# Banks of the second chunk's transposes, an earlier first weight load, a pair of maxima and an addition moved, in a transformer block on one core

## The chip, the cores and the metric

The kernel runs on one core of one Trainium2 chip. The metric is the device time of one execution in microseconds; smaller is better. The core has five engines with a queue each: PE (matrix products; its weight loads, PEld, overlap its matmuls), DVE (vector work), ACT (activations, copies), POOL (GpSimd) and SP, which here issues nearly all DMA transfers. Each engine runs its own queue in order, and an instruction waits until the semaphores that it names are reached. Matmul results go to PSUM, eight banks of 128 partitions by 512 float32.

## What is computed

The reference, cut to the computation (S = 2048 tokens, D = 640, 32 heads of 20, a window of 256 keys, 1728 hidden units):

```python
xn = _layernorm(x, axis=-1)
return x + _A_ref(xn, A_wqkv, A_wo) + _B_ref(xn, B_w_gate, B_w_up, B_w_down)

# _A_ref: sliding-window attention
scores = jnp.einsum("bhqd,bhkd->bhqk", q, k) * (Dh ** -0.5)
mask = (idx[:, None] - idx[None, :] >= 0) & (idx[:, None] - idx[None, :] < W)
scores = jnp.where(mask[None, None], scores, -1e9)
p = _softmax(scores, axis=-1)
o = jnp.einsum("bhqk,bhkd->bhqd", p, v)
return (lambda x, *d: x.transpose(*d))(o, 0, 2, 1, 3).reshape(B, S, D) @ wo

# _B_ref: gated GELU
h = _gelu(g) * u
return jnp.einsum("bsf,fd->bsd", h, w_down)
```

All is float32. The kernel keeps that accuracy by splitting each operand of a product into a high part (rounded to the type that PE reads quickly) and a low part (the rest), and by adding three products: high by high, low by high, high by low. In names, `xh` and `xl` are the two parts of the normalised and transposed x, `wqh`/`wql` and `wvh`/`wvl` those of weights.

## The kernel before

The tokens are cut into four chunks of 512 (c = 0 to 3), each of four tiles of 128. D is cut into KT = 5 blocks of 128 (k). Four phases follow one another.

**The ramp (lines 342 to 470).** For each chunk: load four x tiles (`ln_load`), take their mean and variance on DVE (`ln_stats`, lines 141 to 143), normalise them in place (`ln_apply`, line 161), transpose them block by block on PE (`turn`, line 178), copy the result from PSUM to `xh` on ACT and form `xl` on DVE (lines 186 and 187; 349 and 346 for chunk 0). Then PE makes the first projections of q and k (`proj_qk`, matmul at line 108, into `ps_d`) and those of v (`proj_v`, into `ps_v`) for the chunk. `save_qk` splits a q or k result into three bfloat16 parts (ACT line 274, DVE line 270 into `r`, ACT line 255, POOL line 256) and stores them to DRAM; `save_v` copies v (ACT line 328).

Three PSUM pools are open in this phase: `psd` with two banks (tag "dn"), `psx` with two (tag "ex") and `psm` with four (tag "mx"). A tile takes the next bank of its pool and waits until the last reader of the tile that had it before is done. `turn` takes a letter that picks the pool: "x" for `psx`, "m" and "o" for `psm`. For chunks 1 to 3 `ln_turn` makes all five blocks; its letters alternate, x, m, x, m, x.

In chunk 0 (`first_chunk`) the order of all engines but SP is written by hand, as the code stands. It works on two halves of 256 tokens, `halves[0]` from tiles 0 and 1, `halves[1]` from tiles 2 and 3. `ta` are the transposes of the first half, `tb` those of the second. `high` makes `xh` (ACT), `low` makes `xl` (DVE), `part` issues five matmuls of one product over one half. `wr0` and `wr5` are the raw weights of q tile 0 and k tile 0; `high_qk` makes their high part (ACT, line 358), `low_qk` their low part (POOL, line 363). A copy of one element on POOL makes POOL wait until `xs[3]` is normalised. Ahead of this block PE runs 64 small matmuls on zeros (`warm`). What is not written by hand, such as POOL's memsets of the v tiles, of `ones` and of the mask, is placed by the planner: in the built order of this kernel they stand ahead of `first_chunk`'s POOL work.

For chunk 1 PE's order is written by hand too (lines 442 to 447): VLEAD = 35 matmuls of the v projections of chunk 0 (60 in all) come first, then the 20 transposes of chunk 1, then the other v matmuls.

**Attention (lines 791 to 840).** All engines but SP are in a hand-written order made by a slot loop: 32 units u (8 groups of four heads by 4 chunks), NS = 14 slots each, T counts slots. In each slot come score products and exponentials, row maxima (`max_pair`: products into two `psm` banks, line 509, read by DVE, line 513), products with v (line 595), and a measure of filler matmuls (`pull_fill`: projections for later groups and the gate and up projections). `pull_max(2, T)` takes the next two max pairs from a stream of eight per unit, that is four DVE reductions. Before slot 0 come 12 ramp slots with six such pulls, and then a stretch of filler, `pull_fill(GAP)` with GAP = 16. In the loop, pulls come at slots 0 (twice from unit 1 on), 4 and 8, and one at T = 2.

**Gate and up (lines 866 to 1380)**, and **the last phase (lines 1383 to 1453)**, which makes the output for 256 tokens at a time (p = 0 to 7) in ten steps each. A step adds into seven or so PSUM banks, named 1 to 8 by their role; from p = 1 on, a step has 21 matmuls in the bank order 1, 2, 4, 5, 6, 7, 3 (line 1208). For each step, `split_step` makes the high and low parts of the left operand two steps ahead (ACT, then DVE line 1046, ending in two low parts, "lo"). At the last step of a p (the turn), `split_step` also calls `first_copy` (bank 1 to SBUF, ACT) and `first_add` (bank 2 plus x, DVE), and `drain` adds the other banks to the x tile `xr` and stores the result; the first of its additions for p = 1 to 6 is bank 4's. The next p's matmuls on a bank wait until DVE or ACT has read it.

Of the kernel before, what the change touches and what calls it, by code (L numbers as in the profile page):

```python
# [31 lines left out]
RATE = 34.05  # L32
V1_AT = "gu", 0, 3
VEARLY = 2
VLEAD = 35
POOL_SLOTS = 13, 0, 1, 2, 3, 4, 5, 6, 7
MXD = 6
KSLOT = 9
# [30 lines left out]
def block_kernel(ctx, tc, x, wqk, wv, wgu, wdo, wdl, out):  # L69
# [64 lines left out]
    def ln_load(t, lp):  # L134
        xi = lp.tile([128, D], F32, name="xi", tag="xi", bufs=8)
        nc.sync.dma_start(xi, x[t * 128:(t + 1) * 128, :])
        return xi
# [43 lines left out]
    def ln_turn(t0, xs):  # L181
        n = len(xs)
        cs = slice(t0 * 128, (t0 + n) * 128)
        for k in range(KT):
            ps = turn(k, xs, "xm"[k % 2])
            nc.scalar.activation(xh[:, k, cs], ps, AF.Copy)
            nc.vector.tensor_tensor(out=xl[:, k, cs], in0=ps, in1=xh[:, k, cs].bitcast(F32), op=OP.subtract)

# [153 lines left out]
    def first_chunk(xs, wr0, wr5, lp):  # L342
        halves = slice(0, 256), slice(256, 512)

        def low(k, ps, cs):
            nc.vector.tensor_tensor(out=xl[:, k, cs], in0=ps, in1=xh[:, k, cs].bitcast(F32), op=OP.subtract)

        def high(k, ps, cs):
            nc.scalar.activation(xh[:, k, cs], ps, AF.Copy)

        def part(ps, w, r, cs, first=False, last=False):
            for k in range(KT):
                nc.tensor.matmul(ps[:, cs], w[:, k, :], r[:, k, cs], start=first and k == 0,
                                 stop=last and k == KT - 1, skip_group_check=True)

        def high_qk(raw):
            wh = wp.tile([128, KT, 128], F32R, name="wqh", tag="wqh")
            nc.scalar.activation(wh, raw, AF.Copy)
            return wh

        def low_qk(raw, wh):
            wl = wp.tile([128, KT, 128], F32R, name="wql", tag="wql")
            nc.gpsimd.tensor_tensor(out=wl, in0=raw, in1=wh.bitcast(F32), op=OP.subtract)
            return wh, wl

        with tc.manual_schedule(engines=MANUAL | {mybir.EngineType.Pool}):
            mv = [lp.tile([128, 2, 2], F32, name="mv", tag="mv", bufs=2) for _ in range(2)]
            ln_stats(xs[0], mv[0][:, 0, :], lp)
            ln_stats(xs[1], mv[0][:, 1, :], lp)
            rs = ln_rstd(*ln_sqrt(mv[0], 2, lp), 2, lp)  # L370
            ln_apply(xs[0], mv[0][:, 0, :], rs[:, 0:1])
            ln_apply(xs[1], mv[0][:, 1, :], rs[:, 1:2])
            ln_stats(xs[2], mv[1][:, 0, :], lp)
            ln_stats(xs[3], mv[1][:, 1, :], lp)
            ta = [turn(k, xs[0:2], "xmxmm"[k]) for k in range(KT)]
            dn = [psd.tile([128, C], F32, name="ps_d", tag="dn") for _ in range(2)]
            high(0, ta[0], halves[0])
            wh0 = high_qk(wr0)
            high(1, ta[1], halves[0])
            wh5 = high_qk(wr5)  # L380
            high(2, ta[2], halves[0])
            vb = ln_sqrt(mv[1], 2, lp)
            for k in (3, 4):
                high(k, ta[k], halves[0])
            for k in range(2):
                low(k, ta[k], halves[0])
            rs = ln_rstd(*vb, 2, lp)
            ln_apply(xs[2], mv[1][:, 0, :], rs[:, 0:1])
            ln_apply(xs[3], mv[1][:, 1, :], rs[:, 1:2])
            part(dn[0], wh0, xh, halves[0], True)  # L390
            part(dn[1], wh5, xh, halves[0], True)
            nc.gpsimd.tensor_copy(one[:, 0:1], xs[3][:, 0:1])
            w0, w5 = low_qk(wr0, wh0), low_qk(wr5, wh5)
            tb = [turn(0, xs[2:4], "o")]
            for k in range(2, KT):
                low(k, ta[k], halves[0])
            for k in range(1, KT):
                tb.append(turn(k, xs[2:4], "oxmxm"[k]))
            for k in range(KT):
                high(k, tb[k], halves[1])  # L400
            for k in range(KT):
                low(k, tb[k], halves[1])
            mv = lp.tile([128, 4, 2], F32, name="mv4", tag="mv4", bufs=2)
            part(dn[0], wh0, xl, halves[0])
            part(dn[1], wh5, xl, halves[0])
            part(dn[0], wh0, xh, halves[1])
            part(dn[1], wh5, xh, halves[1])
            for i, w in enumerate((w0, w5)):
                part(dn[i], w[1], xh, halves[0])
                part(dn[i], w[1], xh, halves[1])  # L410
                part(dn[i], w[0], xl, halves[1], last=True)
                for j in range(4 if i == 0 else 0):
                    ln_stats(xs[4 + j], mv[:, j, :], lp)
                save_qk(5 * i, 0, dn[i])
        return w0, w5, mv

    v0 = []
    with tc.tile_pool(name="lp", bufs=1, side="right") as lp:
        xs = [ln_load(t, lp) for t in range(4)]
        warm = lp.tile([128, 256], BF, name="warm")[:, 0:128]  # L420
        nc.vector.memset(warm, 0.0)
        ps = psd.tile([128, C], F32, name="ps_u", tag="dn")
        for i in range(WARM):
            nc.tensor.matmul(ps[:, 0:128], warm, warm, start=True, stop=True)
        wr0, wr5 = load_qk(0), load_qk(5)
        prep = load_v(0, v0, lp)
        next(prep)
        xs += [ln_load(t, lp) for t in range(4, 8)]
        w0, w5, mv1 = first_chunk(xs, wr0, wr5, lp)
        run(prep)  # L430
        v0 = v0[0]
        ones = lp.tile([4, 2 * C], BF, name="ones")
        nc.gpsimd.memset(ones, 0.0)
        nc.gpsimd.memset(ones[0:2], 1.0)
        for i in range(NK):
            for j in (0, 2):
                nc.sync.dma_start(ks[i][SR:64, j:j + 2].rearrange("p j t -> p (j t)"), ones)
        for c in range(1, NC):
            ln_scale(xs[4 * c:4 * c + 4], lp, mv1 if c == 1 else None)
            vs = [proj_v(v0, 4 * c - 4 + i, None if i % 2 else (psm, "mx")) for i in range(4)]  # L440
            if c == 1:
                with tc.manual_schedule(engines={mybir.EngineType.PE}):
                    lead = (cost for gen in vs for cost in gen)
                    for _ in range(VLEAD):
                        next(lead)
                    ln_turn(4 * c, xs[4 * c:4 * c + 4])
                    run(lead)
            else:
                ln_turn(4 * c, xs[4 * c:4 * c + 4])
            if c + 1 < NC:  # L450
                xs += [ln_load(t, lp) for t in range(4 * c + 4, 4 * c + 8)]
            if c == 1:
                for i in range(NQ):
                    for j in (0, 2):
                        nc.sync.dma_start(qs[i][SR + 2:64, j:j + 2].rearrange("p j t -> p (j t)"), ones[2:4])
            if c == 2:
                band = lp.tile([128, D], F32, name="xi", tag="xi", bufs=8)[:, 0:320]
                for t, shift in ((mask, 0), (band, 64)):
                    nc.gpsimd.memset(t, 0.0)
                    nc.gpsimd.affine_select(out=t, in_=t, pattern=[[1, 320]], compare_op=OP.is_ge,  # L460
                                            fill=NEG, base=shift - 1, channel_multiplier=-1)
                    nc.gpsimd.affine_select(out=t, in_=t, pattern=[[-1, 320]], compare_op=OP.is_ge,
                                            fill=NEG, base=256 - shift, channel_multiplier=1)
                nc.gpsimd.tensor_copy(mask[64:128], band[64:128])
                raws1 = [load_qk(1), load_qk(6)]
            if c < NC - 1:
                run(*vs)
                run(proj_qk(0, w0, c), proj_qk(5, w5, c))
            else:
                run(*[proj_v(v0, 4 * c - 4 + i) for i in range(VEARLY)])  # L470
# [320 lines left out]
    def attention():  # L791
# [7 lines left out]
        for i in range(12):  # L799
# [4 lines left out]
                pull_max(2, now[0])  # L804
            flush()
            pull_fill(2 * RAMP)
        pull_fill(GAP)
        for u in range(NU + 1):
            for i in range(NS):
                T = now[0] = NS * u + i  # L810
                for fn, a in tick():
                    fn(*a)
                if i in (0, 4, 8) or T == 2:
                    pull_max(2, T)
                if i == 0 and u:
                    av_unit(u - 1)
# [405 lines left out]

    def first_add(ps, xt):
        sub(xt[:, 1, 0:HD], ps[2][:, 0:HD], xt[:, 1, 0:HD], OP.add)

    puts = []

    def drain(p, ps, xt):
# [21 lines left out]
        if p == NP - 1:  # L1250
# [13 lines left out]
            add(1, 2, b[3])  # L1264
            store(1, 2)
            return
        add(2, 1, b[4])
        sub(q, b[6], a, OP.add)
        add(1, 2, q)
        sub(q, b[7], q, OP.add)  # L1270
# [226 lines left out]
```

## Time and profile before

| | |
|---|---|
| time, median of 3 runs | 1053.38 us (1052.72 to 1054.26) |
| the profiled execution | 1051.12 us |
| its span in the trace | 1049.4 us |
| DVE, ACT, POOL busy | 730.4, 515.1, 333.4 us |
| maxima on DVE (line 513) | 512, 474 ns each |
| DMA, read and written | 101.78 MB, 54.92 MB |

The profile is of one execution. Each row of its timeline has a start, a duration (of all instructions of the row together), the engine, the source line, the operation, output and inputs by the program's names, the shape and the count; in square brackets stands how long the engine was idle before it and what ended the idle time. Rows merge instructions of one line, so a row of 16 transposes is 16 instructions. A matmul's end is modelled and includes its latency, so consecutive rows of PE overlap a little; for the pace of PE one takes the distance between starts. A wait for several semaphores is put down to the one that came last by the trace.

### The profile page before, as it was taken

How to read it: one execution, taken by the hardware profiler on the slowest of the kernel's cores; microseconds unless marked ns; L12 is line 12 of the kernel's file. 1: busy time of each engine (PE TensorE's matmuls, PEld its weight loads, DVE VectorE, ACT ScalarE, POOL GpSimd, SP SyncE). 2: the span in 40 equal slices, each digit the busy share in tenths (PEclk: the TensorE clock that was granted, in tenths of full speed). 3: DMA queues.
4: the chain of work that ended last, by engine and by line, in shares of the span. 5: the costliest groups of instructions: out<-in, count | busy, mean ns of one | idle time of the engine just before them, and what ended most of it. 6: DMA issues, size and time to landing. Idle time of an engine off the chain costs nothing.

```text
span 1049.4 us, 22713 instructions
## 1 busy us (share of the span) xinstructions
PE 1037.5 (99%) x7997; PEld 826.7 (79%) x7997; DVE 730.4 (70%) x2007; ACT 515.1 (49%) x1088; POOL 333.4 (32%) x502
## 2 busy tenths in 40 slices
PE   8999999999999999999999999999999999999998
PEld 7887666666677766666666888888888999999998
DVE  8745656666665556677672677877656889888887
ACT  4434667666665566656555622222334554333332
POOL 5121676867373548373735011110110000000000
PEclk9999999999999999999999999999999999999999
DMA  6543455655443244444322656676317874443442
GB/s 212 181 118 97 122 154 157 180 170 168 119 127 98 85 116 142 152 124 136 107 84 67 196 186 243 211 251 239 119 51 256 267 247 136 132 130 112 126 136 92
DMA packets 105179, 158.56 MB, mean 151 GB/s; under 512 B 15420, under 2 KB 60092, under 8 KB 105064
## 3 DMA queue, kind: packets, MB, share of 16 engines
q1 hardware_dynamic: 102680, 150.95, 45.5%
q10 hardware_dynamic: 2384, 6.16, 1.9%
q8 instruction: 63, 1.03, 0.4%
q14 instruction: 52, 0.43, 0.1%
HBM read 101.78 MB, written 54.92 MB: 149 GB/s over the span
## 4 chain that ended last, share of the span: by engine, by line
PE 93%; DVE 4%; issue 1%; DMA 1%; ACT 1%; POOL 0%; SPq 0%; DVEq 0%; POOLq 0%
PE ps_d L108 21%; PE ps L1208 21%; PE ps_g L941 21%; PE ps_e L568 8%; PE ps_o L595 8%; PE ps_v L108 6%; PE ps_m L509 5%; PE ps_g L108 1%; DVE xi L161 1%; DVE st L142 1%; DVE st L141 1%; DVE ss L1046 0%; DVE junk L513 0%; DVE r L270 0%; DMA qs<-qd 0%
## 5 line engine op out<-in xcount | busy, mean ns | idle before, releaser
L513 DVE CUSTOM_DVE_ANT_0 junk<-ps_m,mask 128x320 bf16<-128x320 f32 (+2 forms) x512 | 242.9, 474 | 146.5 <-PE ps_m L509 88.2
L570 ACT ACTIVATE P<-ps_e 128x512 f32<-128x512 f32 (+2 forms) x384 | 198.2, 569 | 66.4 <-PE ps_e L568 62.0
L1208 PE MATMUL ps<-wb,at 128*128 128x320 f32 x999 | 155.9, 309 | 0.0
L1208 PEld LDWEIGHTS ps<-wb,at 128*128 128x128 f32 x999 | 148.9, 188 | 0.2
L581 POOL TENSOR_SCALAR_AFFINE_SELECT P<-P 128x512 f32<-128x512 f32 x128 | 83.5, 652 | 153.3 <-ACT P L570 153.3
L568 PE MATMUL ps_e<-qs,ks 124*128 124x128 bf16 (+2 forms) x704 | 117.3, 278 | 0.3 <-ACT ob L599 0.2
L108 PE MATMUL ps_d<-xh,wqh 128*128 128x512 f32 x350 | 107.8, 416 | 0.0
L108 PE MATMUL ps_d<-xl,wqh 128*128 128x512 f32 x350 | 107.5, 415 | 0.0
L108 PE MATMUL ps_d<-xh,wql 128*128 128x512 f32 x350 | 107.2, 414 | 0.0
L1208 PE MATMUL ps<-wt,at 128*128 128x320 f32 x552 | 89.1, 309 | 0.5 <-DVE xr L1233 0.5
L568 PEld LDWEIGHTS <-ks 124*128 124x128 bf16 x704 | 49.4, 98 | 48.0 <-issue 33.6
L595 PE MATMUL ps_o<-P,v 128*32 128x384 f32 (+2 forms) x1408 | 84.3, 386 | 0.0
L1208 PEld LDWEIGHTS ps<-wt,at 128*128 128x128 f32 x552 | 82.9, 188 | 0.9 <-DVE xr L1233 0.7
L1162 ACT ACTIVATE at<-ss 128x512 fp32r<-128x512 f32 x59 | 37.3, 632 | 89.3 <-DVE ss L1046 89.3
L584 POOL TENSOR_SCALAR_AFFINE_SELECT P<-P 128x512 f32<-128x512 f32 x112 | 72.7, 659 | 25.1 <-ACT P L570 25.1
L101 POOL TENSOR_TENSOR wql<-wr,wqh 128x640 fp32r<-128x640 f32 x11 | 17.6, 1607 | 174.8 <-PE ps_g L941 129.4
L108 PEld LDWEIGHTS ps_d<-xh,wql 128*128 128x128 f32 x350 | 64.2, 189 | 10.5
L108 PEld LDWEIGHTS ps_d<-xl,wqh 128*128 128x128 f32 x350 | 64.1, 189 | 10.4 <-issue 0.2
L108 PEld LDWEIGHTS ps_d<-xh,wqh 128*128 128x128 f32 x350 | 63.7, 189 | 10.4 <-issue 0.3
L595 PEld LDWEIGHTS ps_o<-P,v 128*32 128x32 f32 x1408 | 41.3, 110 | 38.6 <-issue 21.9
L256 POOL TENSOR_TENSOR pt<-r,pt 128x512 bf16<-128x512 f32 x40 | 46.8, 1170 | 66.7 <-ACT pt L255 52.6
L509 PE MATMUL ps_m<-ks,qs 60*64 60x320 bf16 (+2 forms) x1472 | 62.2, 260 | 2.1 <-DVE mx L513 1.0
(193 smaller groups left out, 1808.0 us busy)
## 6 DMA issues: line engine op xcount, KB each, us to landing
hr<-hd SPq DMA_DIRECT2D x104, 128.0 KB
hd<-he SPq DMA_DIRECT2D x50, 256.0 KB
wr<-wgu SPq DMA_DIRECT2D x27, 320.0 KB
qs<-qd SPq DMA_DIRECT2D x64, 120.0 KB
ks<-kd SPq DMA_DIRECT2D x64, 120.0 KB
xi<-x SPq DMA_DIRECT2D x16, 320.0 KB
qs<-qd SPq DMA_DIRECT2D x64, 80.0 KB
ks<-kd SPq DMA_DIRECT2D x64, 80.0 KB
```

What stands on the lines that cost most here:

```text
L108: nc.tensor.matmul(ps, a(k), b(k), start=n == 0, stop=n == 3 * nk - 1)
L256: nc.gpsimd.tensor_tensor(out=pt[:, l, :], in0=r, in1=pt[:, 1, :], op=OP.subtract)
L509: nc.tensor.matmul(ps[64 * h:64 * h + 64, lo:hi], q[rows, j, q0:q0 + 64], keys, start=True, stop=True, tile_position=(64 * r, 64 * h))
L513: nc.vector.tensor_tensor_reduce(out=junk[:, 0:n], in0=ps[:, 0:n], in1=mask[:, 320 - n:320], scale=1.0, scalar=NEG, op0=OP.add, op1=OP.max ...
L568: nc.tensor.matmul(ps[:, col:col + n], k[0:QROWS, j, kc:kc + 128], q[0:QROWS, j, q0:q0 + n], start=True, stop=True)
L570: nc.scalar.activation(pt[:, j, lo:hi], ps[:, lo:hi], AF.Exp, scale=SCALE)
L581: nc.gpsimd.affine_select(out=a, in_=a, pattern=[[0, 4], [1, 128]], compare_op=OP.is_ge, fill=0.0, base=0, channel_multiplier=-1)
L584: nc.gpsimd.affine_select(out=a, in_=a, pattern=[[0, 4], [-1, 128]], compare_op=OP.is_ge, fill=0.0, base=-1, channel_multiplier=1)
L595: nc.tensor.matmul(o[32 * j:32 * j + 32, q0:q0 + n], v[:, w0_:w0_ + 32], pt[:, j, col:col + n], start=i == 0, stop=i == len(todo) - 1, ski ...
L941: nc.tensor.matmul(ps, i, j, start=first and n == 0, stop=n == len(work) - 1, skip_group_check=True)
L1162: nc.scalar.activation(hi[:, 3:7], s, AF.Copy)
L1208: nc.tensor.matmul(ps[bank][:, 0:HD], *work[bank][j], start=bank not in begun, stop=final[p, bank] == n and j == len(work[bank]) - 1, skip ...
```

## The change

Four edits, in one diff:

1. `ln_turn` picks the pools by "xmmxm" instead of x, m, x, m, x, and VLEAD goes from 35 to 40.
2. The load of `wr0` is issued after the first two x tiles instead of after four. In `first_chunk`, `wh0` is made (ACT) ahead of the `xh` copies and `w0`'s low part (POOL) right behind it, after a one-element copy that makes POOL wait for `xs[1]`; `wh5` comes after the fourth `xh` copy. The product of `w0`'s low part with the first half is issued second instead of late.
3. One `pull_max(2)` moves from T = 2 to the middle of the gap ahead of slot 0.
4. In the last phase the addition of bank 4 moves from the start of `drain` to `first_add`, that is ahead of the two low parts of `split_step`.

```diff
-VLEAD = 35
+VLEAD = 40
...
-            ps = turn(k, xs, "xm"[k % 2])
+            ps = turn(k, xs, "xmmxm"[k])
...
             ln_stats(xs[3], mv[1][:, 1, :], lp)
+            nc.gpsimd.tensor_copy(one[:, 0:1], xs[1][:, 0:1])
+            wh0 = high_qk(wr0)
+            w0 = low_qk(wr0, wh0)
             ta = [turn(k, xs[0:2], "xmxmm"[k]) for k in range(KT)]
             dn = [psd.tile([128, C], F32, name="ps_d", tag="dn") for _ in range(2)]
             high(0, ta[0], halves[0])
-            wh0 = high_qk(wr0)
-            high(1, ta[1], halves[0])
+            for k in range(1, 4):
+                high(k, ta[k], halves[0])
             wh5 = high_qk(wr5)
-            high(2, ta[2], halves[0])
             vb = ln_sqrt(mv[1], 2, lp)
-            for k in (3, 4):
-                high(k, ta[k], halves[0])
+            high(4, ta[4], halves[0])
...
             part(dn[0], wh0, xh, halves[0], True)
+            part(dn[0], w0[1], xh, halves[0])
             part(dn[1], wh5, xh, halves[0], True)
             nc.gpsimd.tensor_copy(one[:, 0:1], xs[3][:, 0:1])
-            w0, w5 = low_qk(wr0, wh0), low_qk(wr5, wh5)
+            w5 = low_qk(wr5, wh5)
...
             for i, w in enumerate((w0, w5)):
-                part(dn[i], w[1], xh, halves[0])
+                if i:
+                    part(dn[i], w[1], xh, halves[0])
                 part(dn[i], w[1], xh, halves[1])
...
-        xs = [ln_load(t, lp) for t in range(4)]
+        xs = [ln_load(t, lp) for t in range(2)]
+        wr0 = load_qk(0)
+        xs += [ln_load(t, lp) for t in range(2, 4)]
...
-        wr0, wr5 = load_qk(0), load_qk(5)
+        wr5 = load_qk(5)
...
-        pull_fill(GAP)
+        pull_fill(GAP / 2)
+        pull_max(2, now[0])
+        pull_fill(GAP / 2)
...
-                if i in (0, 4, 8) or T == 2:
+                if i in (0, 4, 8):
                     pull_max(2, T)
...
     def first_add(ps, xt):
         sub(xt[:, 1, 0:HD], ps[2][:, 0:HD], xt[:, 1, 0:HD], OP.add)
+        sub(xt[:, 0, 0:HD], ps[4][:, 0:HD], xt[:, 0, 0:HD], OP.add)
...
-        add(2, 1, b[4])
         sub(q, b[6], a, OP.add)
```

In the built order of the changed kernel, the one-element copy and `w0`'s low part stand on POOL ahead of the memsets of the v tiles, `ones` and the mask. On SP, the x tiles 10 and 11 are loaded behind the stores of the first q and k results (before, tile 11 alone), and each of the second weight loads comes behind a pair of stores. On DVE, two of chunk 2's tiles have their statistics ahead of chunk 1's `xl`, and two behind them.

## The prediction, made before the changed kernel was run

> **What bounds the kernel now.** I read the page first, then busy time by stage, then the waits of PE, then the timeline at each place that an edit touches.
>
> ```profile
> span 1049.4 us, 22713 instructions
> ...
> PE 1037.5 (99%) x7997; PEld 826.7 (79%) x7997; DVE 730.4 (70%) x2007; ACT 515.1 (49%) x1088; POOL 333.4 (32%) x502
> ...
> PE 93%; DVE 4%; issue 1%; DMA 1%; ACT 1%; POOL 0%; SPq 0%; DVEq 0%; POOLq 0%
> ```
>
> ```profile
> 0.00:13.50 13.50, 9.51 (x85) 8.05 (x85) 9.29 (x32) 6.62 (x16) 6.27 (x24) 1.00 0.83 303
> ...
> 25.70:33.30 7.60, 6.14 (x48) 5.81 (x46) 7.27 (x21) 3.68 (x11) 0.00 (x0) 1.00 0.53 144
> ...
> 65.00:110.00 45.00, 44.09 (x347) 33.76 (x349) 23.80 (x94) 18.37 (x55) 12.24 (x13) 1.00 0.39 117
> 110.00:820.00 710.00, 708.52 (x5711) 513.71 (x5704) 464.85 (x1363) 377.25 (x780) 299.68 (x450) 1.00 0.48 152
> ```
>
> The first fence has the span, the engines and the chain's shares of the page; the second has stages (start:end, length, then busy us of PE, PEld, DVE, ACT, POOL, granted clock, DMA share, GB/s). PE is 99% busy and 93% of the chain that ended last, at full clock. Both kernels have the same number of matmuls, so only idle PE time can be won: span less PE's busy time is 11.9 us. Four of them lie ahead of 13.5 us, 1.5 in 25.7 to 33.3 (which ends where the first ps_d of chunk 1 starts), 0.9 in 65 to 110, 1.5 in the next 710. What ended that idle time:
>
> ```profile
> PE ps_t L178 <- DVE xi L161: 1.9, 2, 1.2
> PE ps_t L178 <- DVE xl L187: 1.5, 1, 1.5
> ...
> PE ps_m L509 <- DVE mx L513: 1.0, 3, 0.4
> PE ps_m L509 <- DMA qs<-qd: 0.9, 1, 0.9
> ...
> PE ps L1208 <- DVE xr L1233: 0.5, 1, 0.5
> ...
> PEld ps_t L178 <- DVE xl L187: 2.4, 3, 1.7
> ```
>
> Columns: us in total, times, longest. The four edits touch the waits on xl, xi, mx and xr.
>
> **Edit 1, the banks (ln_turn, VLEAD).** Before, the five transposes of a chunk alternate between pool x (two banks) and pool m, so k=4 needs k=0's bank and waits for DVE's xl of k=0. With "xmmxm" x serves k=0 and 3, m serves k=1, 2 and 4. These three and the two v projections in m are five uses of four banks; the one used twice in chunk 1 is that of the first v tile, which ACT has saved long before. So the wait goes in chunks 1, 2 and 3:
>
> ```profile
> 25.70 1.97 PE L178 MATMUL ps_t<-ident,xi 128*128 128x128 f32 x16
> ...
> 29.14 0.42 PEld L178 LDWEIGHTS ps_t<-ident,xi 128*128 128x128 f32 x4 [1.70 <-DVE xl L187]
> ...
> 42.41 0.42 PEld L178 LDWEIGHTS ps_t<-ident,xi 128*128 128x128 f32 x4 [0.35 <-DVE xl L187]
> ```
>
> The weight-load side gives the fuller stall, since a matmul's modelled end includes its latency: 1.70 + 0.35, and by the total of 2.4 for three another 0.35 in chunk 3. Bounds: 1.5 (PE's own row) to 2.4 gained; I take **-2.4**, because PE's next instruction starts when its weights are in. VLEAD 40 puts five more v matmuls ahead of chunk 1's transposes, 0.147 us each (35 of them from 20.57, a row below, to 25.70): 0.73 moved, not added. What is late next is DVE's normalising of chunk 1, done at 25.98 (23.48 + 2.50 below), and the five matmuls cover it. In chunks 2 and 3 the second v projection now asks for a bank that DVE frees with r; in DVE's order that r comes ahead of xl of k=0, the very wait removed, and PE has the rest of the transposes and 15 matmuls (2.2 us) ahead of it: nothing added.
>
> **Edit 2, the first weights.** On SP the load of wr0 goes ahead of x tiles 2 and 3; ACT makes wqh0 before the xh copies; POOL waits for xs[1] (the one-element copy), makes wql0, and only then runs the memsets and masks it used to run at the start; five wql0 matmuls (first half) move ahead of xs[3].
>
> ```profile
> 13.53 1.20 PE L178 MATMUL ps_t<-ident,xi 128*128 128x128 f32 x9 [0.74 <-DVE xi L161]
> 16.97 1.36 PE L353 MATMUL ps_d<-xh,wql 128*128 128x256 f32 x10
> 18.17 0.76 PE L353 MATMUL ps_d<-xl,wqh 128*128 128x256 f32 x5
> 20.57 0.90 PE L108 MATMUL ps_v<-wvh,xh 128*128 128x320 f32 x5
> ```
>
> ```profile
> 1.79 0.11 POOL L309 MEMSET v<- 128x12 f32 x1
> ...
> 3.61 0.94 POOL L434 MEMSET ones<- 2x1024 bf16 x1
> ...
> 5.02 0.45 POOL L462 TENSOR_SCALAR_AFFINE_SELECT mask<-mask 128x320 f32<-128x320 f32 x1
> ...
> 15.12 3.10 POOL L363 TENSOR_TENSOR wql<-wr,wqh 128x640 fp32r<-128x640 f32 x2
> ```
>
> Ten wql matmuls take 18.17 - 16.97 = 1.20, so five are worth 0.60, and PE sits idle for 0.74 just ahead of xs[3]: they fit. POOL pays for it. xs[1] is ready at 8.18 (7.05 + 1.13 below) and wql0 lasts 1.55 (half of 3.10), so it is done at 9.9; the memsets and the first mask step take 5.02 - 1.79 = 3.2, to 13.1; three wvl, the second mask step and the gate follow, and wql5 is done at about 18.3. PE asks for it at 18.17 (five wql0 fewer, the five xl now ahead of it): a wait of 0.1. That leaves -0.5.
>
> Against it, the moved POOL work now lies under DVE's two normalising steps of tiles 2 and 3:
>
> ```profile
> 7.05 1.13 DVE L161 TENSOR_SCALAR xi<-xi,mv,rs 128x640 f32<-128x640 f32 x2
> ...
> 11.79 1.68 DVE L161 TENSOR_SCALAR xi<-xi,mv,rs 128x640 f32<-128x640 f32 x2
> ...
> 21.44 1.17 POOL L256 TENSOR_TENSOR pt<-r,pt 128x512 bf16<-128x512 f32 x1 [1.54 <-ACT pt L255]
> 21.48 1.48 DVE L161 TENSOR_SCALAR xi<-xi,mv,rs 128x640 f32<-128x640 f32 x1
> ...
> 23.48 2.50 DVE L161 TENSOR_SCALAR xi<-xi,mv,rs 128x640 f32<-128x640 f32 x3
> ```
>
> ```profile
> 99.72 0.64 POOL L584 TENSOR_SCALAR_AFFINE_SELECT P<-P 128x512 f32<-128x512 f32 x1
> ...
> 100.11 0.27 DVE L522 TENSOR_SCALAR nm<-mx 128x16 bf16<-128x16 f32 x1
> ```
>
> Alone, two steps take 1.13. Behind POOL's 1.17 one step takes 1.48 and ends 0.35 after POOL's op; the small tensor_scalar at 100.11 ends at 100.38, with POOL's select (100.36). No row shows a POOL memset under such a step. If it blocks nothing, the two steps take 1.13 instead of 1.68 and -0.5 stands. If it blocks as the select does, the first step waits for the 0.90 of ones (11.74 to 12.64), the second for a select, and they end at about 14.2 instead of 13.47; POOL slips too, wql5 is done at about 18.95, and PE reaches the v projections at 18.95 + 0.05 + 15 x 0.12 = 20.8 against 20.57: +0.25. DVE's chunk 1 is then ready at 26.7, and PE starts its transposes at 25.70 + 0.25 + 0.73 = 26.7. A memset is nearest to the select's row: I take **+0.1**, toward that end; bounds -0.6 and +1.0 (each step behind a 0.9 us op, and wql5 late by as much).
>
> [...]
>
> Late elsewhere, at no cost: x tiles 2 and 3 come behind 320 KB more, but DVE asks for tile 2 only after 8.18. The eight ks<-ones transfers stand on SP until the later memset of ones (12.6 instead of 4.55), and x loads of chunk 2 queue behind them and behind the q and k stores; DVE asks for two of those tiles at 25.98, for the other two only after the xl of chunk 1. If that cover failed, chunk 2's normalising would be late by what the tiles miss.
>
> **Edit 3, the pair of maxima.** One pull (two pairs) moves from slot T=2 to the middle of the gap, where DVE is idle.
>
> ```profile
> 94.69 0.47 PE L509 MATMUL ps_m<-ks,qs 60*64 60x64 bf16 x16
> 95.07 0.49 DVE L513 CUSTOM_DVE_ANT_0 junk<-ps_m,mask 128x320 bf16<-128x320 f32 x1 [4.63 <-PE ps_m L509]
> ...
> 96.70 0.51 PE L509 MATMUL ps_m<-ks,qs 60*64 60x320 bf16 x5
> ...
> 97.56 0.33 PE L509 MATMUL ps_m<-ks,qs 60*64 60x320 bf16 x3 [0.35 <-DVE mx L513]
> ...
> 100.13 0.33 PE L509 MATMUL ps_m<-ks,qs 60*64 60x128 bf16 x7 [0.28 <-DVE mx L513]
> ```
>
> Three pulls fall within 5 us, DVE lags, and PE waits 0.35 + 0.28. After, the third comes 5 us after the second, so 0.28 goes. The first two are then 12 v matmuls and the pull's own 0.47 apart, 2.2 us against 2.0 now, so about 0.15 of the 0.35 stays. **-0.45**; bounds -0.63 and +0.3 (the wait stays, with one more like it).
>
> **Edit 4, the addition.** add(2,1,b4) goes ahead of DVE's two lo splits at six turns; at one of them PE waits now:
>
> ```profile
> 901.90 2.22 PE L1208 MATMUL ps<-wt,at 128*128 128x320 f32 x12 [0.46 <-DVE xr L1233]
> ...
> 902.87 0.49 DVE L1046 TENSOR_TENSOR u<-ps,u 128x320 f32<-128x320 f32 x1
> ...
> 903.42 0.45 PEld L1208 LDWEIGHTS ps<-wt,at 128*128 128x128 f32 x3 [0.20 <-DVE u L1046]
> ```
>
> Bank 4 comes free about 1 us earlier, so the 0.46 goes. But DVE has the same work ahead of its read of bank 7 (902.87), which ends at 903.36 as now, and PE, at bank 7 earlier, waits there until 903.42: the stall moves by nine matmuls, its end stands. **0**; bounds -0.46 and +0.1. The lo splits come one addition later; the 21 matmuls of a whole step (3.1 us) stand ahead of their use.
>
> **Sum**: -2.4 + 0.1 - 0.45 + 0 = -2.75 us. The profiled execution took 1051.12 (span 1049.4, 1.7 around it), 2.26 under the median 1053.38; the three timed runs spread over 1.5 us. Span 1046.65, that execution 1048.4, median **1050.6 us** (-0.26%). After 110 us PE's progress releases nearly everything else, so I expect it to keep its lead.
>
> **Rivals.** (a) POOL takes the gain of the ramp: its ops block both normalising steps and wql5 is late, +1.0 instead of +0.1, and chunk 1's transposes wait 0.4 more for DVE. Gain 1.45: 1051.9. For: 1.48 behind 1.17. Against: at 11.79, with POOL's wvl beneath, DVE lost only 0.55 over its two steps (1.68 against 1.13).
> (b) The bank stall is hidden anyway: PE gains 1.7 in chunk 1 and loses it again behind DVE's r and xl, which the first maxima need. Gain 1.05: 1052.3. For: DVE is busy 7.27 of 7.60 there. Against: in 65 to 110 DVE is busy only half the time.
> (c) Slower: the stack loads (qs<-qd) keep their time while PE is 2.75 ahead, so that maxima find their data late. It decides from the fourth further wait of 0.9 on; six make +5.4, net +2.65: 1056.0. For: one such wait exists. Against: it is alone among 32 units, and the loads are released by PE's own progress.
>
> Chances: forecast 0.62, (a) 0.2, (b) 0.11, (c) 0.07. The measurement tells 0.2% (2.1 us) from no change: the forecast counts as faster, (a) and (b) as within it. Range: the low ends together, -0.6 - 2.4 - 0.63 - 0.46 = -4.1, give 1049.3; (b) with 0.4 of spread gives 1052.7.
>
> **What would show it.** Right: no wait of ps_t on xl; five wql matmuls ahead of xs[3]; the first ps_d of chunk 1 at about 31.6 instead of 33.3; no wait at T=4; at the turn near 899 one wait of about 0.7 on bank 7 in place of two. L161 near 12 us decides on the memsets: 1.1 for the pair without a lock, over 2 with it, and then the second wql group waits for POOL. Wrong: PE's idle time after 110 us grows by over 1 us, or that ps_d starts after 32.5.

## The result, and the profile after

The changed kernel took **1047.88 us** (median of 6 runs, 1047.34 to 1048.98), before in the same comparison 1053.79 (6 runs, 1052.72 to 1054.88): ratio 0.9945, 95% interval 0.9932 to 0.9958. The forecast was 1050.6, its range 1049.3 to 1052.7: right in sign, but the measured time lies 1.4 us below the range. The profiled executions stand closer together, 1051.12 before and 1047.46 after. So there are two questions: why the trace shows 3.7 us instead of the 2.75 of the sum, and where the other 2.2 us between 3.7 and 5.9 are.

The page of the changed kernel, its span, busy times and the chain's shares:

```profile
span 1045.7 us, 22718 instructions
...
PE 1035.9 (99%) x7997; PEld 826.6 (79%) x7997; DVE 730.8 (70%) x2007; ACT 514.7 (49%) x1088; POOL 333.6 (32%) x503
...
PE 96%; DVE 2%; DMA 1%; ACT 0%; issue 0%; SPq 0%; DVEq 0%
```

Its stages, columns as before:

```profile
0.00:13.50 13.50, 9.41 (x90) 8.31 (x90) 9.26 (x31) 6.79 (x16) 6.35 (x24) 1.00 0.83 302
...
25.70:31.23 5.53, 5.53 (x45) 5.52 (x44) 5.50 (x13) 3.10 (x9) 0.22 (x1) 1.00 0.65 194
65.00:110.00 45.00, 44.64 (x359) 33.68 (x358) 25.15 (x97) 20.28 (x56) 12.50 (x13) 1.00 0.39 119
110.00:820.00 710.00, 708.82 (x5701) 515.87 (x5700) 465.38 (x1356) 375.22 (x777) 299.52 (x449) 1.00 0.48 152
```

What PE waited for (total, times, longest):

```profile
PE ps_t L178 <- DVE xi L161: 2.4, 3, 1.5
...
PE ps_m L514 <- DMA qs<-qd: 0.6, 1, 0.6
PE ps L1215 <- DVE u L1053: 0.4, 1, 0.4
PE ps_m L514 <- DVE mx L518: 0.4, 1, 0.4
```

No wait on xl is left, the waits on mx fell from 1.0 to 0.4, and that on xr became one on u. The waits on xi rose from 1.9 to 2.4, of which 0.3 is only that the warm-up row ended earlier (1.48 idle behind it instead of 1.17) while the first transposes start where they did (7.84 and 7.81). PE has no idle time from 25.7 to 31.23; the stretch from 110 to 820 is as full as before. Its timeline in the ramp (start, duration, instruction):

```profile
11.21 0.75 PE L353 MATMUL ps_d<-xh,wql 128*128 128x256 f32 x5
...
13.17 0.33 PE L178 MATMUL ps_t<-ident,xi 128*128 128x128 f32 x1 [0.62 <-DVE xi L161]
...
20.26 0.90 PE L108 MATMUL ps_v<-wvh,xh 128*128 128x320 f32 x5
...
26.13 2.34 PE L178 MATMUL ps_t<-ident,xi 128*128 128x128 f32 x20
...
31.23 1.32 PE L108 MATMUL ps_d<-xh,wqh 128*128 128x512 f32 x5
```

The five wql matmuls stand at 11.21, ahead of the transposes of xs[2] and xs[3]; the 20 transposes of chunk 1 run in one piece; the first ps_d of chunk 1 starts at 31.23. Landmarks along PE, from the two timelines, us:

| where | before | after | lead |
|---|---|---|---|
| v projections start | 20.57 | 20.26 | 0.31 |
| first ps_d of chunk 1 | 33.30 | 31.23 | 2.07 |
| first ps_m | 65.23 | 62.56 | 2.67 |
| first ps_n | 86.16 | 83.46 | 2.70 |
| pull at T=14 (slot 0 of unit 1) | 108.23 | 104.46 | 3.77 |
| end of the span | 1049.4 | 1045.7 | 3.7 |

Edits 1 and 2 give 2.7 by 63 us, edit 3 gives 1.07 between 86 and 108, and from there on the lead stays.

### The profile page after: what moved, and what is told of

Read it like the earlier page. It is cut to its first block, busy times and chain, and to the rows that moved or that the text cites. A ratio compares the mean times of both kernels' runs of the same rounds, so it can differ in the third digit from the quotient of the medians.

```text
span 1045.7 us, 22718 instructions
## 1 busy us (share of the span) xinstructions
PE 1035.9 (99%) x7997; PEld 826.6 (79%) x7997; DVE 730.8 (70%) x2007; ACT 514.7 (49%) x1088; POOL 333.6 (32%) x503
## 4 chain that ended last, share of the span: by engine, by line
PE 96%; DVE 2%; DMA 1%; ACT 0%; issue 0%; SPq 0%; DVEq 0%
PE ps_d L108 23%; PE ps_g L948 21%; PE ps L1215 21%; PE ps_e L573 9%; PE ps_o L600 8%; PE ps_v L108 7%; PE ps_m L514 5%; PE ps_g L108 1%; PE ps_t L178 1%; PE ps_d L353 1%; DVE ss L1053 0%; DMA qs<-qd 0%; DVE at L1053 0%; DVE xi L161 0%; DMA xi<-x 0%
## 5 line engine op out<-in xcount | busy, mean ns | idle before, releaser
L604 ACT ACTIVATE ob<-ps_o 128x512 f32<-128x512 f32 x32 | 19.1, 597 | 88.9 <-PE ps_o L600 77.6
```

## The experiments

Each kernel was timed beside before on one chip, in four comparisons: base_again, e1_banks, e2_weights and e3_pull in the first; after_again, without_e2, before_filled and e4_add in the second; after_third and ones_first in the third; load_order and filled_again in the fourth. "Clock" is the mean granted clock of TensorE that each run lists; the last two columns are the share of runs at 0.999 or more and the median of these. The ratio is the record's estimate with its interval, not the quotient of the two medians. Before's share differs much from one comparison to the next, so shares are best compared within one.

| kernel | median us (runs) | ratio to before, 95% | at 0.999 or more | their median |
|---|---|---|---|---|
| before, four comparisons | 1053.53, 1052.58, 1053.26, 1052.07 (35, 29, 12, 23) | | 51 of 99 (14 of 35, 21 of 29, 3 of 12, 13 of 23) | 1051.88 |
| base_again | 1052.38 (12) | 0.9988, 0.9977 to 0.9999 | 8 of 12 | 1051.66 |
| e1_banks | 1050.53 (12) | 0.9972, 0.9959 to 0.9985 | 5 of 12 | 1049.59 |
| e2_weights | 1051.74 (12) | 0.9981, 0.9969 to 0.9993 | 11 of 12 | 1051.69 |
| e3_pull | 1051.74 (12) | 0.9981, 0.9968 to 0.9994 | 5 of 12 | 1050.55 |
| e4_add | 1053.32 (12) | 1.0004, 0.9992 to 1.0016 | 8 of 12 | 1051.98 |
| without_e2 | 1050.48 (11) | 0.9975, 0.9963 to 0.9986 | 4 of 11 | 1047.78 |
| after_again | 1048.62 (5) | 0.9956, 0.9942 to 0.9970 | 5 of 5 | 1048.62 |
| after_third | 1048.91 (7) | 0.9960, 0.9945 to 0.9974 | 6 of 7 | 1048.61 |
| ones_first | 1049.50 (5) | 0.9959, 0.9947 to 0.9972 | 4 of 5 | 1049.16 |
| before_filled | 1052.49 (11) | 0.9999, 0.9988 to 1.0010 | 10 of 11 | 1052.41 |
| filled_again | 1052.94 (12) | 0.9996, 0.9983 to 1.0010 | 9 of 12 | 1052.10 |
| load_order | 1052.92 (12) | 1.0005, 0.9993 to 1.0017 | 6 of 12 | 1052.26 |

**base_again: before, unchanged.**

> The kernel before, unchanged, to see what a further execution of it looks like. The profiled execution of before took 1051.12 us, under all six of its timed runs (1052.72 to 1054.88), so the two profiles differ by 3.7 us where the medians differ by 5.9. Theory 1 (the profiled execution of before lacked a stall that a typical one has): a second profile is 1052.5 to 1054.5 and shows 2 us more of idle PE at one place or a few. Theory 2 (a profile of this kernel is always about 2 us under its timed runs): a second profile is again near 1051 with the same waits of PE. Ratio to before: 1.000.

The unchanged copy came out at 0.9988. A ratio nearer to 1 than about 0.0012 is therefore scatter here. Its profiled execution took 1051.37 with the same waits, as in Theory 2; but a profiled execution is not always the shorter one (that of e4_add took 1055.55, its median is 1053.32). The longer runs mostly go with a lower clock, which is taken up below.

**e1_banks: edit 1 alone.**

```diff
-VLEAD = 35
+VLEAD = 40
-            ps = turn(k, xs, "xm"[k % 2])
+            ps = turn(k, xs, "xmmxm"[k])
```

> Edit 1 alone: the letters xmmxm and VLEAD 40. By the terms of the trace it gains 2.1 to 2.4 us (the three waits on xl): 1051.4 to 1051.7 against 1053.8. If what the typical run of before has over its profile lies in these waits, 4 to 4.6 us: 1049.3.

Timelines of PE, first base_again, then e1_banks: the first ps_d of chunk 1 and the first ps_m.

```profile
33.39 1.32 PE L108 MATMUL ps_d<-xh,wqh 128*128 128x512 f32 x5
...
65.33 0.36 PE L509 MATMUL ps_m<-ks,qs 60*64 60x64 bf16 x12
```

```profile
26.53 2.35 PE L178 MATMUL ps_t<-ident,xi 128*128 128x128 f32 x20
...
31.64 1.32 PE L108 MATMUL ps_d<-xh,wqh 128*128 128x512 f32 x5
...
62.96 0.36 PE L509 MATMUL ps_m<-ks,qs 60*64 60x64 bf16 x12
```

1.75 in chunk 1 and 2.37 by the first ps_m, against 2.4 forecast. At 0.999 or more its runs are 2.07 under the copy's.

**banks_only and vlead_only: its two halves** (one of the diff's two lines each). Each ran once, under the profiler: 1051.27 and 1051.36 us, both at a clock of 0.998.

> Edit 1 without its VLEAD part (35 as before). Theory (the bank is the whole stall, VLEAD only covers DVE's normalising): no wait of ps_t on xl; PE asks for chunk 1's transposes at 25.8, DVE is done at 26.0, so at most 0.3 us of wait on xi comes in; the first ps_d of chunk 1 starts at 31.6 to 31.9, against 33.4 in before's copy and 31.64 with both parts. Rival (VLEAD carries part of the gain): 32.2 or later.

> The other part of edit 1 alone (VLEAD 40, banks as before). DVE's xl of k=0 stands behind statistics of later tiles until 28.5, whenever PE's transposes come, so the stall on it ends at 29.2 as in before; but five v matmuls (0.73 us) are then ahead of it instead of behind. Theory: the wait of ps_t on xl shrinks from 1.5 to about 0.8, the first ps_d of chunk 1 starts at 32.6 to 32.9 instead of 33.4. Rival (the stall only moves, as the transposes come later): 33.3 or later.

In both executions the clock dropped ahead of this place (below), so distances from the start of the v projections are compared. PE of banks_only, then of vlead_only:

```profile
21.92 0.90 PE L108 MATMUL ps_v<-wvh,xh 128*128 128x320 f32 x5
...
27.05 2.34 PE L178 MATMUL ps_t<-ident,xi 128*128 128x128 f32 x20
...
32.90 1.32 PE L108 MATMUL ps_d<-xh,wqh 128*128 128x512 f32 x5
```

```profile
22.20 0.90 PE L108 MATMUL ps_v<-wvh,xh 128*128 128x320 f32 x5
...
30.57 0.66 PE L178 MATMUL ps_t<-ident,xi 128*128 128x128 f32 x4 [0.59 <-DVE xl L187]
...
33.99 1.32 PE L108 MATMUL ps_d<-xh,wqh 128*128 128x512 f32 x5
```

banks_only needs 10.98 from the v projections to ps_d, as e1_banks does (31.64 - 20.66), with no wait on xl: in these executions the banks are the whole gain. The times in its expectation were those of full clock and did not come. But PE came 1.3 us late to the transposes, so whether VLEAD is needed to cover DVE's normalising at full clock was not seen. vlead_only needs 11.79, base_again 12.73. e3_pull, which has the old banks, VLEAD 35 and the same lateness, needs 12.33 (34.61 - 22.28): VLEAD alone is worth some 0.5, the low end of the 0.5 to 0.8 expected, though DVE's xl moved with the lateness (29.88 instead of 28.51), which the expectation had excluded.

**e2_weights: edit 2 alone** (its lines of the diff).

> Edit 2 alone: wr0 loaded third, wql0 ahead of the memsets, its first-half product moved up. By the trace of after PE reaches the v projections 0.31 us earlier: 0.3 us of gain, not to be told from none (1053.5); the wait of 1.5 us on xl stays. If the missing 2 us are this edit's, 1051.3.

At full clock 1051.69, level with the copy, so a gain of 0.3 can't be told from none; by its trace the v projections start at 20.29 instead of 20.66. Its clock share, 11 of 12, stands out.

**e3_pull: edit 3 alone.**

```diff
-        pull_fill(GAP)
+        pull_fill(GAP / 2)
+        pull_max(2, now[0])
+        pull_fill(GAP / 2)
...
-                if i in (0, 4, 8) or T == 2:
+                if i in (0, 4, 8):
```

> Edit 3 alone: the pull of two pairs from T=2 to the middle of the gap. The trace of after against before gains 0.9 us between the last ramp pull and the first ob copy, against 0.45 forecast: 1052.9. If DVE's backlog of maxima is worse in a typical run of before than in its profile, up to 3 us: 1050.8.

From the first ps_n to the pull at T=14 it takes 21.00 (87.47 to 108.47), the copy 22.08 (86.26 to 108.34): 1.08 gained, as in the changed kernel.

**e4_add: edit 4 alone.**

```diff
         sub(xt[:, 1, 0:HD], ps[2][:, 0:HD], xt[:, 1, 0:HD], OP.add)
+        sub(xt[:, 0, 0:HD], ps[4][:, 0:HD], xt[:, 0, 0:HD], OP.add)
...
-        add(2, 1, b[4])
```

> Edit 4 alone: the addition from bank 4 moved ahead of the first writes. Theory: the wait of 0.4 us on bank 4's reader is gone and the next one, on bank 7's reader, takes its place with 0.4 us, so the time at 1.000 is before's (1051.4 to 1052.0) and about half of the runs are at 1.000. Rival: the wait vanishes and the kernel is 0.4 us shorter at 1.000 (1051.3 or less).

PE at the turn near 900 waits on bank 7's reader and on nothing else, and the time at full clock is that of before:

```profile
905.69 1.73 PE L1208 MATMUL ps<-wt,at 128*128 128x320 f32 x9
907.84 0.71 PE L1208 MATMUL ps<-wt,at 128*128 128x320 f32 x3 [0.42 <-DVE u L1046]
```

**ones_first: the changed kernel with the two memsets of ones ahead of POOL's wait.**

```diff
+            nc.gpsimd.memset(ones, 0.0)
+            nc.gpsimd.memset(ones[0:2], 1.0)
             nc.gpsimd.tensor_copy(one[:, 0:1], xs[1][:, 0:1])
...
-        nc.gpsimd.memset(ones, 0.0)
-        nc.gpsimd.memset(ones[0:2], 1.0)
```

> The changed kernel with the two memsets of ones ahead of POOL's wait for xs[1]. In the changed kernel's profile DVE's two normalising steps for tiles 2 and 3 (L161 near 11.8) take 1.96 us; the first lies beside the memset of ones (11.82 to 12.76), the second beside the select of mask (12.74 to 13.43). Theory (a POOL memset holds back such a step): with ones out of the way the pair takes at most 1.7 (as in before, with wvl beneath it), the transposes of xs[2] start at 12.5 to 12.7 instead of 13.17, the v projections 0.2 to 0.4 earlier (19.9 to 20.1 instead of 20.26), and the profiled execution, if its clock is 1.000, is 0.2 to 0.4 shorter than the changed kernel's, too little for the medians to tell. Rival (memsets block nothing, the pair is slow for another reason): 1.9 to 2.0 again, transposes at 13.1 to 13.2.

DVE's and POOL's timelines in the changed kernel, then in ones_first:

```profile
11.81 1.96 DVE L161 TENSOR_SCALAR xi<-xi,mv,rs 128x640 f32<-128x640 f32 x2
...
11.82 0.94 POOL L439 MEMSET ones<- 2x1024 bf16 x1
12.74 0.69 POOL L465 TENSOR_SCALAR_AFFINE_SELECT mask<-mask 128x320 f32<-128x320 f32 x1
```

```profile
11.87 2.28 DVE L161 TENSOR_SCALAR xi<-xi,mv,rs 128x640 f32<-128x640 f32 x2
...
11.86 1.94 POOL L299 TENSOR_TENSOR wvl<-wvall,wvh 128x320 fp32r<-128x320 f32 x2 [0.58 <-ACT wvh L298]
```

A miss: the pair took 2.28, not 1.7, and the v projections start at 20.64, not at 19.9 to 20.1. With the memsets gone, wvl moved up into their place, 0.01 us ahead of DVE. Memset, select or wvl, the outcome is the same: of the changed kernel's pair, the first step ends at 13.12 (1.31 long), 0.36 after the memset, and the second at 13.77, 0.34 after the select; the pair in ones_first ends 0.35 after the second wvl (14.15 against 13.80). So the memset held back such a step here, and so did the select and wvl: the pairs took 1.96 and 2.28, against 1.13 with no POOL work beside them (7.05 in before). In before the pair took 1.68: its first step began 0.2 ahead of wvl and took 0.61, and only the second, 1.16 long, was held.

**The clock.** The next three kernels ask where the 2.2 us between trace and medians are.

> All four edits, timed beside before on one chip. Each run lists the mean clock granted to TensorE. At 1.000, before took 1051.9 (median of 13 runs) and its unchanged copy 1051.7 (8 runs); a run at 0.998 or below was some 2 us longer. Theory (clock): the edits save 3.7 us of work, which is what the two profiled executions differ by (both at 1.000), and the rest of the 5.9 us between the medians is runs of before whose clock fell in the ramp. So at 1.000 this kernel takes 1047.8 to 1048.4, 3.5 to 3.9 less than before at 1.000, and at least 8 of 12 runs are at 1.000, against 13 of 35 of before: the three kernels without edit 2 had 18 of 36 at 1.000, edit 2 alone 10 of 12. Rival A (the gain is larger than the profile shows): also at 1.000 the two are 5.5 to 6 us apart. Rival B (the clock is chance of the day, no edit touches it): 4 to 6 of 12 at 1.000, and the medians of all runs 3.7 apart.

> Edits 1, 3 and 4 without edit 2 (first weights loaded and split as before). Theory (clock by edit 2): about half of the runs at 1.000, as before; at 1.000 the kernel takes 1048.2 to 1048.7, that is the 0.3 us by which edit 2 brings the v projections forward more than all four edits; median over all runs 1049.3 to 1050.5. Rival (edit 2 has nothing to do with the clock): share at 1.000 and median as of the kernel with all four, within 0.4 us.

> Before, with 24 matmuls of the zero warm-up tile put into the three idle stretches of TensorE between 9.5 and 13.6 us (4 of them in the 0.23 us, 8 in the 0.51 us, 12 in the 0.74 us; 0.056 us each by the warm-up row), nothing else changed. One profile with a clock of 0.998 shows where it fell: 0.50 from 14 to 17 us, one stretch of about 3.4 us, right behind these idle stretches. Theory (the clock falls because TensorE idles there): at 1.000 in at least 9 of 12 runs, time at 1.000 unchanged (1051.4 to 1052.0), median of all runs there too, 0.5 to 1.5 us below before's. Rival (the fall has another cause, or these gaps are too small a share): 4 to 6 of 12 at 1.000, median as before's, 1052.4 to 1053.5.

Where the clock fell, in e3_pull (mean 0.998), by stages; the clock is the third number from the end:

```profile
12.00:14.00 2.00, 1.25 (x10) 0.94 (x9) 2.00 (x4) 1.44 (x5) 1.91 (x2) 0.99 0.47 177
14.00:15.00 1.00, 1.00 (x7) 1.00 (x6) 1.00 (x4) 0.92 (x3) 1.00 (x2) 0.50 0.11 27
...
16.00:17.00 1.00, 1.00 (x7) 1.00 (x6) 1.00 (x4) 0.02 (x1) 1.00 (x2) 0.50 0.79 202
17.00:18.00 1.00, 1.00 (x9) 1.00 (x9) 0.96 (x4) 0.00 (x0) 1.00 (x1) 0.81 0.77 200
```

By these means, with the clock taken as either 1.00 or 0.50 (0.99 is 0.04 us at half clock, 0.81 is 0.38), PE runs at half clock from 13.96 to 17.38; the v projections start at 22.28 instead of 20.66. e4_add (13.04 to 19.86, worked out in the same way), banks_only and vlead_only show the drop at the same place, and these four are all the profiled executions below 0.999 of kernels without fillers. Over all runs, 87 of 172 without edit 2 and without fillers were at 0.999 or more, with edit 2 32 of 35. Before's runs below it take 1054.03 (48 runs), those above 1051.88 (51): **2.15 us**. after_again missed its expected 1047.8 to 1048.4 by 0.2; without_e2 reached 1047.78 at full clock, below its expected 1048.2 to 1048.7, so the 0.3 of edit 2 does not show in the times there; over all runs it took 1050.48, because 7 of its 11 fell below.

before_filled put 24 zero matmuls into PE's idle stretches (4 after the first transposes, 8 after the second wqh matmul, 12 between the transposes of xs[2] and xs[3]). The clock held in 10 of 11 (before beside it: 21 of 29), but no time was won. So the gain, the clock and edit 2's halves were asked once more.

> The changed kernel once more, beside before on the same chip, for the two open numbers. The gain: 4 us between the medians (3.2 to 4.8), as in the second comparison (1052.58 and 1048.62), not 5.9. The clock: with edit 2 in the kernel 22 of 23 runs so far were granted 0.999 or more, without it 65 of 123 (before and its variants); so at least 10 of 12 here, and 15 to 22 of some 30 of before. Rival: shares alike.

> Before with the load of wr0 moved ahead of x tiles 2 and 3 and nothing else of edit 2: ACT, POOL and TensorE in the old order. So far 32 of 35 runs with the whole of edit 2 were granted 0.999 or more, and 68 of 137 without it. Theory (what keeps the clock is TensorE's new order around 9.5 to 13.6 us: four matmuls without a gap, five wql matmuls ahead of xs[3]): about half at 0.999 or more, as without edit 2, and the v projections start where they did in the copy of before (20.6 to 20.9 at full clock). Rival (the load order alone does it, through what the DMAs or ACT do there): at least 9 of 12.

> Before with the 24 zero matmuls in TensorE's three idle stretches, once more: 10 of 11 runs were at 0.999 or more, but their median was 0.5 us above that of before's runs at such a clock, and the overall median no lower than before's. Theory (the idle stretches cause the drop, and the 0.5 us was scatter): at least 9 of 12 again, median 0.5 to 1.3 us below before's of the same chip. Rival 1 (10 of 11 was chance): 5 to 7 of 12. Rival 2 (the fillers keep the clock and cost as much as they save): at least 9 of 12, and the median within 0.3 us of before's.

after_third: the medians differ by 4.35, clock at 1.000 in 6 of 7, 3 of 12 of before. load_order, the new load order alone: 6 of 12, as without edit 2, so the load order alone does not do it. filled_again: 9 of 12, and the median 0.9 above before's. Together the fillers' runs are at 0.999 or more in 19 of 23, and before's beside them, on the same two chips, in 34 of 52: not clear of chance. These 19 take 1052.33, 0.45 above before's. That is nearest to Rival 2 (they save nothing), though the median of 12 lies outside the 0.3 it allowed. Whether idle PE time in the ramp bears on the clock is therefore not shown. What it is in edit 2's order that holds the clock stays **open** as well: by PE's rows the changed kernel idles there no less (0.69 + 0.62 + 0.32) than before (0.23 + 0.51 + 0.74).

## Why the prediction was right or wrong

Two steps failed. The larger is the last step of the sum, from one profiled execution to the median: 2.26 us were added to the changed kernel as to before, and its own median stands only 0.42 above its profiled execution. The other is the price of edit 3. Of the 2.7 between the forecast and the median, about 1.8 come from the first and 0.6 from the second; edit 2, mis-sized too, gave 0.4. Edits 1 and 4 came as forecast.

**Edit 1 was right.** Forecast -2.4, measured -2.37 by the first ps_m with edit 1 alone. Reading the stall on the weight-load side (1.70 instead of PE's 1.46) was right: chunk 1 gave 1.75. Rival (b) is out.

**Edit 2 was too dear by 0.4.** Forecast +0.1, measured -0.31 at the v projections. The reading of the memsets was right in kind: the step beside one took 1.31, and the pair 1.96 (1.68 in before). But it ended at 13.77, not at 14.2, and that is all it cost: 0.60 of matmuls moved ahead, less the 0.30 by which the pair ends later (13.47 before), is the 0.31. POOL's slip, which I had put on the path as well, lay under PE's own arrival: wql5 was done at 18.25, and PE reached it at 18.46. Both timelines above agree that such a step is held beside POOL's work, a memset included: it took 1.31 beside the memset of 0.94 and ended 0.36 after it, and the other held steps ended 0.34 and 0.35 after the select and the second wvl. What holds it there is not shown. Rival (a) had the blocking right and its price wrong: both steps were held, but the pair ended only 0.30 later than in before, against 0.60 moved ahead.

**Edit 3 failed: forecast -0.45, measured -1.07.** I priced its waits by PE's idle column, 0.35 and 0.28, right after having shown in edit 1 that this column understates a stall, and put a third place at nothing. The better measure is from a pull's start to the start of what follows. PE of before, with ACT's read of ps_n, then PE of the changed kernel (each pull, and the instruction behind it):

```profile
97.82 0.50 PE L568 MATMUL ps_e<-qs,ks 124*128 124x384 bf16 x2
...
99.47 0.38 PE L509 MATMUL ps_m<-ks,qs 60*64 60x64 bf16 x9
...
100.40 0.39 PE L568 MATMUL ps_e<-qs,ks 124*128 124x256 bf16 x2
...
102.96 0.23 PE L530 MATMUL ps_n<-identb,nm 128*128 128x128 bf16 x1
103.12 0.75 PE L509 MATMUL ps_m<-ks,qs 60*64 60x320 bf16 x8
103.22 0.27 ACT L532 ACTIVATE mr<-ps_n 32x128 bf16<-32x128 f32 x1 [0.45 <-PE ps_n L530]
103.80 0.61 PE L568 MATMUL ps_e<-qs,ks 124*128 124x128 bf16 x4
```

```profile
92.59 0.84 PE L514 MATMUL ps_m<-ks,qs 60*64 60x320 bf16 x8
93.36 0.50 PE L573 MATMUL ps_e<-qs,ks 124*128 124x384 bf16 x2
...
96.51 0.47 PE L514 MATMUL ps_m<-ks,qs 60*64 60x64 bf16 x16
96.91 0.39 PE L573 MATMUL ps_e<-qs,ks 124*128 124x256 bf16 x2
...
98.31 0.23 PE L535 MATMUL ps_n<-identb,nm 128*128 128x128 bf16 x1
...
99.62 0.47 PE L514 MATMUL ps_m<-ks,qs 60*64 60x320 bf16 x8
100.02 0.62 PE L573 MATMUL ps_e<-qs,ks 124*128 124x128 bf16 x4
```

The second pull behind the ramp (T=2 in before, T=0 now that one pull stands in the gap) went from 1.12 (96.70 to 97.82) to 0.77: 0.35 where I had counted 0.2. The pull at T=4 went from 0.93 to 0.40: 0.53 for 0.28. The one at T=8 went from 0.68 to 0.40: 0.28 for nothing. Sum 1.16, of which 1.07 is left at T=14.

The first two are DVE's backlog of maxima. The third is another wait, in a row that reads 0.75 instead of 0.47 and lists none. In before ps_n, the transpose of the finished maxima, comes directly ahead of the pull at T=8 and takes one of the four psm banks; ACT reads it until 103.49, and the last two matmuls of the pull start at 103.54, while DVE had been idle since 102.93. At 87.06 in the same trace the same order is listed as a wait of 0.28 on ACT's mr. The code calls ps_n six slots after the pull that finishes the maxima, so with that pull at T=0 instead of T=2 it comes at T=6 (98.31), and the pull at T=8 is free of it. That ACT's read held PE is read from these times; no run tests it by itself.

**Edit 4 was right**: 0, and one wait on bank 7 in place of the one on bank 4. On the changed kernel's weight-load side (the timeline near 899):

```profile
899.76 0.44 PEld L1215 LDWEIGHTS ps<-wt,at 128*128 128x128 f32 x3 [0.68 <-DVE u L1053]
```

0.68, as the forecast's "about 0.7" had it. From the 30 matmuls ahead of the turn to the nine behind it PE takes 7.09 in both kernels (896.87 to 903.96 and 893.21 to 900.30): the stall moved and its end stood.

**From 3.7 to 5.9: the step to the median failed, as the sum was made against one execution at full clock.** The profiled execution of before stood 2.26 below the median, and I carried this offset over to the changed kernel as if it were fixed. It was not. Two further comparisons gave 4.0 (1052.58 and 1048.62) and 4.35 (1053.26 and 1048.91); over all 99 runs of before and 18 of the changed kernel the medians are 1052.81 and 1048.22, 4.6 apart, and at 0.999 or more 1051.88 and 1048.14 (17 of the 18), 3.74 apart. So 3.7 is work; about 0.9 more goes with the clock drop, which half of before's runs have and one of 18 of the changed kernel's; and the remaining 1.3 up to 5.9 did not come back in the other two comparisons and has no cause shown. That edit 2 is the part that holds the clock is shown by shares (32 of 35 runs with it, 87 of 172 without; e2_weights alone 11 of 12, before beside it 14 of 35), though the second comparison says less (after_again 5 of 5, without_e2 4 of 11, before 21 of 29); how it does so is not shown.

**Rival (c)** did not come: the wait for stack loads is 0.6 in the changed kernel, 0.9 in before. Longer waits on them do occur as scatter: e1_banks waited 1.5, ones_first 1.8.

## What to carry to other kernels

Price a stall from the start of the waiting group to the start of the next instruction, in every term and not only in the largest, and look at the groups after it for rows that are longer than the same row elsewhere: a wait can hide there unlisted (at T=8 in before the row reads 0.75 instead of 0.47), and it can be on another engine than the backlog that one is looking at. Before adding a forecast saving to a median, see whether the profiled execution's granted clock and time are typical of the runs; where runs differ in clock, an edit's effect on the share of undisturbed ones is a term of its own. An operation moved off one engine's start lands beside another's work: what counted here is which pair then overlapped, for a normalising step of DVE ended 0.34 to 0.36 us after a memset, a select or a wvl of POOL alike.

## What the runs showed of the hardware

In the profiled executions the clock drop in the ramp goes with the length of the warm-up row, 64 equal matmuls. It took 6.13 to 6.58 us in the four executions that dropped there, and 5.92 or less in every other execution profiled (5.20 in the changed kernel). The row holds two paces: before, with a row of 5.47, has 12 matmuls between 2 and 3 us, 14 between 4 and 5 and 22 between 5 and 6, the changed kernel, with 5.20, has 12, 19 and 22. Of these two the longer row has the later step to the quicker pace, and the clock is granted at 1.00 in all these stretches. And row and drop move together: with rows of 6.13, 6.22, 6.34 and 6.58 (e4_add, banks_only, vlead_only, e3_pull) the drop begins at 13.04, 13.22, 13.47 and 13.96, each time twice the row plus 0.78 to 0.80. The row of e3_pull:

```profile
1.17 6.58 PE L424 MATMUL ps_u<-warm 128*128 128x128 bf16 x64 [1.17 <-DVE warm L421]
```

The low stretch lasts 3.42 us in e3_pull, as long in banks_only (13.22 to 16.64) and 3.41 in vlead_only (13.47 to 16.88), all worked out as above, and 6.82, twice that, in e4_add. What sets its start and its length, and why the same kernel drops in some runs and not in others, is not shown. The executions with edit 2 all had warm-up rows of at most 5.83, so none shows its order behind a row as long as those four.

The clock also fell once far from the ramp, in filled_again, behind two late stack loads: PE, then the stages with the clock third from the end.

```profile
161.17 0.19 PE L521 MATMUL ps_m<-ks,qs 60*64 60x64 bf16 x1 [1.16 <-DMA qs<-qd]
162.00 0.47 PE L521 MATMUL ps_m<-ks,qs 60*64 60x64 bf16 x15 [0.65 <-DMA qs<-qd]
```

```profile
160.00:162.00 2.00, 0.19 (x2) 0.13 (x2) 0.69 (x1) 0.44 (x1) 1.96 (x3) 1.00 0.67 194
162.00:163.00 1.00, 1.00 (x19) 0.76 (x20) 0.50 (x2) 0.27 (x1) 0.07 (x1) 0.89 0.86 224
163.00:164.00 1.00, 1.00 (x4) 0.81 (x3) 0.84 (x3) 0.39 (x2) 0.00 (x0) 0.50 0.26 94
```

By such means the half clock lasts from 162.8 to 166.2, 3.4 us once more. So 1.8 us of waits on these loads (1.16 + 0.65) were followed by 3.4 us at half clock in this one execution; that the waits caused the drop is not shown, and waits on these loads need not be followed by one: e4_add waited 1.8 us on them (the longest 1.1), ones_first 1.8 (1.1) and e1_banks 1.5 (1.1), and the mean clock of the whole execution is 1.000 in ones_first and e1_banks; in e4_add it is 0.997, which the 6.82 us in the ramp make up alone (3.41 of 1053.8).
